# Linear attention followed by an MLP: the place of batch 3's v casts and key products inside chunk 2

## The chip, the cores and the metric

The kernel runs on one core of one Trainium2 chip. The metric is the device time of one execution in microseconds (us), median of several. A profile of one execution accompanies it: for every instruction it has the engine, the start, the length and what released it. Engines are named as in the profile: PE is TensorE's matmuls, PEld its weight loads, DVE is VectorE, ACT is ScalarE, POOL is GpSimd, SP is SyncE, which here only issues DMAs.

## The reference

Eight batches of eight heads, 576 rows, 64 columns a head. Attention without a square matrix: q is normalised by a softmax along its columns, k by a softmax along the sequence, and the product of k and v (64x64 for a head) is applied to q. The heads side by side give x (576 rows of 512), on which a layer norm, two matrix products with a ReLU between them and the residual follow.

```python
q_s = softmax(q, axis=-1)
k_s = softmax(k, axis=2)
kv  = einsum('bhsd,bhse->bhde', k_s, v)
x   = einsum('bhsd,bhde->bhse', q_s, kv)     # heads side by side: (8, 576, 512)
xn  = (x - mean(x)) / sqrt(var(x) + 1e-6) * g_ln
out = x + maximum(xn @ w_ch1, 0) @ w_ch2     # 512 -> 2048 -> 512
```

## The kernel before

**Chunks.** The MLP runs over chunks: chunk c is the first 512 rows of batch c, for c from 0 to 7, and a ninth chunk holds the remaining 64 rows of all eight batches. `mlp_steps(c)` gives the MLP of a chunk as a list of small TensorE steps, each with a weight, and `run(main, side)` (L846) issues them in order. `side` is a list of (position, function): before the main step at which the summed weight reaches that position, the function is issued. So the order on every engine is written out by hand, with positions from 0 to 112 in a chunk. A semaphore is waited for wherever an instruction needs another engine's result, and each engine takes its instructions strictly in that order.

**What is beside what.** While chunk c's MLP runs, the side list holds the attention of batch c + 1 (`attn_fast`, L877) and the loads and exponentials of batch c + 2 (`load_batch`, `load_v`, `prep_fast`).

**First product of a chunk** (`mm1_fast`, L753; chunks 2 and later). A Strassen-like scheme with seven products in place of eight. The 16 blocks of the hidden width are taken as four groups, two at a time. For each pair of groups the products come in the order 1, 5, 6, 2, 7, 3, 4; each has 4 matmuls for a group and weighs 2, so a pair takes 28 of the chunk's positions, and the two pairs take 0 to 56. Products 1, 6, 7 and 4 of a group share one PSUM bank (`bx`), 5 and 3 another (`bb`), 2 a third (`bc`), which begins as a copy of `bx`. Between them stand short operations:

- after product 5, ScalarE copies `bb` to SBUF (`s`, L778)
- after product 6, VectorE adds `bx` and `s` into `bb` (`add_5`, L781); product 7 writes `bx` again and so waits for it
- after product 7, VectorE adds `bx` and `s` into the hidden layer (`out_22`, L784), and after the second group of the pair it applies the ReLU to both (L789); product 4 writes `bx` again and so waits for L784
- after products 2, 3 and 4, ScalarE writes the ReLU of the bank to the hidden layer (L792)

Products 5, 6, 7 and 4 take differences of the transposed x, `tq`, which GpSimd forms (`sum_x`, L235 to L247) from `xnT` once a DMA has transposed `xn` (L255).

**Second product of a chunk** (`mm2_fast`, L684; positions 56 to 112), the same scheme over the hidden layer, with sums `hs` that VectorE forms (`sum_h`, L567).

**The attention of a batch.** `load_v(b)` (L139) loads v as bf16 into `vt`, of which there is one buffer, by a DMA on GpSimd's queue, and the remaining 64 rows into `vr`. `cast_v(b, j)` (L131) copies one half of the heads of `vt` into `vm`, where each head has a 65th column of ones, and which has one half for even and one for odd batches. `kv_all(b)` (L396) does the key products: `kv_mm` (L367) issues 40 matmuls of 64x65 into the PSUM tile `pkv`, the first 20 for heads 0 to 3, the others for heads 4 to 7; the 65th column is the sum that the softmax of k divides by. Then `kv_out` (L386) issues on VectorE a reciprocal (L390) and two multiplies (L392) that write `kv_sb`. From position 48 on `po_mm` (L417) multiplies q with it.

**Batch 3.** In most batches one cast is done by VectorE and one by ScalarE at the end of the chunk ahead. For batch 3 `load_v` is issued late in chunk 1 (L899), and both casts are done by VectorE in chunk 2, at positions 4 and 5 (L1186); its `kv_all` is at position 14 (L880), where that of later batches is at 12. `load_v(4)` is at position 26 of chunk 2 (L1183).

Of the kernel before, what the change touches and what calls it, by code (L numbers as in the profile page):

```python
# [20 lines left out]
def kernel(  # L21
# [109 lines left out]
    def cast_v(b, j, eng=None):  # L131
        hs = slice(4 * j, 4 * j + 4)
        dst = vm[:, b % 2, :, hs, 0:D].rearrange("p t h d -> p h t d")
        if eng is nc.scalar:
            nc.scalar.copy(dst, vts[b][:, hs])
        else:
            nc.vector.tensor_copy(out=dst, in_=vts[b][:, hs])
# [39 lines left out]
    def prep_kvrem(b):  # L177
        nc.scalar.activation(ekr[:, b % 2], raws[b][3], AF.Exp)
# [28 lines left out]
    def reduce_q(c, t, tn=1):  # L207
        ts = slice(t, t + tn)
        nc.vector.reduce_sum(eqs[c][1][:, ts], eqs[c][0][:, ts], axis=AX.X)  # L209
# [52 lines left out]
    def xn_T(c, t0, tn):  # L262
        dma_T(xnTs[c], xs[c][2][:, t0 : t0 + tn].rearrange("p t n -> p (t n)"), t0, tn)
# [103 lines left out]
    def kv_mm(b, ts):  # L367

        par = b % 2
        if ts.start == 0:  # L370
            kvbox["p"] = att_ps.tile([P, NP, P], FP32, tag="a", name="pkv")
        pkv = kvbox["p"]
        for jh, t in [(jh, t) for jh in range(2) for t in ts]:
            for j in (2 * jh, 2 * jh + 1):
                for half, ps in enumerate(halves):
                    h = 2 * j + half
                    if t < T:
                        lhsT, rhs = eks[b][:, t, h, :], vm[:, par, t, h, :]
                    else:
                        lhsT, rhs = ekr[:, par, h % 4, :], vr[:, par, h, :]  # L380
                    nc.tensor.matmul(  # L381
                        pkv[ps, j, 0:VW], lhsT, rhs, start=(t == 0 and j == 0), stop=(t == T),
                        skip_group_check=True,
                    )

    def kv_out(b):  # L386

        pkv = kvbox["p"]
        rzk = sml.tile([P, NP], FP32, tag="rzk", name="rzk")
        nc.vector.reciprocal(rzk, pkv[:, :, D])  # L390
        for ps in halves:
            nc.vector.tensor_mul(  # L392
                kv_sb[ps, b, :, ps], pkv[ps, :, 0:D], rzk[ps].to_broadcast([64, NP, D])
            )

    def kv_all(b):  # L396
        kv_mm(b, range(T + 1))
        kv_out(b)

    def start_x(c):  # L400
        xs[c] = (
            mlp.tile([P, T, DM], BF16, tag="x", name="x"),
            mlp.tile([P, T, 6], FP32, tag="st", name="st"),
            mlp.tile([P, T, DM], BF16, tag="xn", name="xn", bufs=1),
            mlp.tile([P, T, 2], FP32, tag="mv", name="mv"),
        )
        xnTs[c] = mlp.tile([P, T, KO1, P], BF16, tag="xnT", name="xnT")
# [36 lines left out]
    def x_fast(c, t, centre=True):  # L444

        x, _, _, mv = xs[c]
        nc.vector.scalar_tensor_tensor(  # L447
            x[:, t].rearrange("p (h d) -> p h d", h=H),
            in0=pobox[c, t].rearrange("p (h d) -> p h d", h=H), scalar=1.0,
            in1=eqs[c][2][:, t].to_broadcast([P, H, D]), op0=ALU.mult, op1=ALU.mult,  # L450
            accum_out=mv[:, t, 0:1],
        )
        if centre:
            xn_out(c, t)
# [387 lines left out]
    def spread(fns, a, b):  # L842
        n = len(fns)
        return [(a + (b - a) * i / n, fn) for i, fn in enumerate(fns)]
# [29 lines left out]
    def recip_q(c):  # L874
        nc.vector.reciprocal(eqs[c][2], eqs[c][1])

    def attn_fast(c):  # L877

        s = [(1, lambda: reduce_q(c, 0, 2)), (27, lambda: reduce_q(c, 2, 2)), (28, lambda: recip_q(c))]
        s += [(14 if c == 3 else 12, lambda: kv_all(c))]  # L880
        s += [(40, lambda: start_x(c))]
        for t, (p0, p1) in enumerate(((48, 53), (57, 59), (65, 67), (73, 75))):
            s += spread([lambda t=t, i=i: po_mm(c, t, i) for i in range(NP)], p0, p1)
            s += [(p1, lambda t=t: x_fast(c, t)), ((66, 74, 87, 91)[t], lambda t=t: square_sum(c, t))]
        s += [(61, lambda: xn_T(c, 0, 2)), (78, lambda: xn_T(c, 2, 2)), (95, lambda: rstd_op(c))]
        if c == C9 - 1:
            return s + [(100, lambda i=i: sum_x(c, i)) for i in range(2)]
        s += [((84, 88, 92, 101)[i], lambda i=i: sum_x(c, i)) for i in range(4)]
        return s
# [231 lines left out]
    with tc.manual_schedule(  # L1121
        engines={mybir.EngineType.PE, mybir.EngineType.DVE, mybir.EngineType.Activation,
                 mybir.EngineType.SP, mybir.EngineType.Pool}
    ):
        first_batch()
        load_behind(1, (2,))
        load_w2(8, 2)
        load_behind(1, (0,))
        load_w2(10, 2)
        load_behind(1, (1,))  # L1130
        load_w2(12, 2)
        load_w2(14, 2)
        load_behind(2)

        def po_x(c, t):
            for i in range(NP):
                po_mm(c, t, i)
            x_fast(c, t)

        run(  # L1140
            mlp_steps(0),
            [
                (2, lambda: (q0_rest(2), x_fast(0, 2))),
                (2.5, lambda: (eq_pT(0, 3, nc.scalar), x_plain(0))),
                (6, lambda: (q0_rest(3), x_plain(1))),
                (7.5, lambda: (xn_pT(0, 2, nc.vector), x_fast(0, 3))),
                (16, lambda: xn_pT(0, 3, nc.vector)),
                (22, lambda: square_sum(0, 0)),
                (26, lambda: square_sum(0, 1)),
                (30, lambda: square_sum(0, 2)),  # L1150
                (34, lambda: square_sum(0, 3)),
                (38, lambda: rstd_op(0)),
            ]
            + [(70, lambda: exp_q(1, 0, 4)), (72, lambda: exp_q(1, 2, 4))]
            + [(75 + t, lambda t=t: reduce_q(1, t)) for t in range(T)]
            + [((82, 86, 94, 98)[t], lambda t=t: eq_pT(1, t, nc.scalar)) for t in range(T)]
            + [(84, lambda: nc.vector.reciprocal(eqs[1][2], eqs[1][1]))]
            + [(88, lambda: exp_k(1, 0, 4)), (92, lambda: exp_k(1, 2, 4))]
            + [(26 + 4 * i, lambda i=i: scale_w1(i % KO1, i // KO1)) for i in range(2 * KO1)]
            + [(p, lambda i=i: quarter_w2(i, 0)) for i, p in enumerate((60, 62, 64, 66))]  # L1160
            + [(p, lambda i=i: sum_w1(i, 0)) for i, p in enumerate((80, 84, 88, 92))]
            + [(p, lambda i=i: sum_w1(i, 1)) for i, p in enumerate((96, 98))]
            + [(103 + 0.4 * j, lambda j=j: cast_v(1, j)) for j in range(2)]
            + [(104.5, lambda: prep_kvrem(1))]
            + [(112, lambda: (kv_all(1), start_x(1)))]
            + [(118, lambda: (po_x(1, 0), po_x(1, 1)))]
            + [(123, lambda: xn_pT(1, 0, nc.scalar)), (125, lambda: square_sum(1, 0))]
            + [(124.1, lambda: (po_x(1, 2), po_x(1, 3)))]
            + [(126, lambda: xn_pT(1, 1, nc.scalar)), (127, lambda: square_sum(1, 1))]
        )  # L1170
        for c in range(1, B):
            side = []
            if c == 1:
                side += second_side()
            else:
                if c + 1 < B:
                    side += attn_fast(c + 1)
                else:
                    side += attn_rest()
                    side += [(6 + i, lambda i=i: sum_x(c, i)) for i in (2, 3)]  # L1180
                if c + 2 < B:
                    side += [(1, lambda b=c + 2: load_batch(b))]
                    side += [(26, lambda b=c + 2: load_v(b))]  # L1183
                    side += prep_fast(c + 2)
            if c == 2:
                side += [(4 + j, lambda j=j: cast_v(3, j)) for j in range(2)]  # L1186
            if c == B - 2:
                side += [(1, load_qrem)]
                side += spread([lambda r=r: exp_qrem(r) for r in range(T)], 58, 80)
                side += [(84, lambda: eq_T(C9))]  # L1190
            sums = [(57, 0)] if c == FAST else [(p, i) for i, p in enumerate((30, 41))]
            run(mlp_steps(c), side + [(at, lambda i=i: sum_h(0, i)) for at, i in sums])
        run(mlp_steps(C9), [(33 + 3 * i, lambda i=i: sum_h(0, i)) for i in range(2)])
# [30 lines left out]
```

## Time and profile before

| | |
|---|---|
| runs | 264.39, 264.46, 265.11 us; median 264.46 us |
| profiled execution | 266.13 us, of which the span from first to last instruction is 264.3 us |
| granted TensorE clock | 1.000 of full speed |
| VectorE, ScalarE, GpSimd busy | 218.0, 180.8, 78.3 us |
| DMA | 45.00 MB, mean 170 GB/s |
| chunk 2, first to last of its TensorE work | 76.49 to 104.78 us |
| chunk 3 | 104.78 to 130.99 us |

The page has the busy time of each engine (matmuls are pipelined, each is given its modelled length of 0.27 us for 128x256 although the next one starts 0.11 us later), the chain of work that ended last, and the costliest groups of instructions. The trace behind it answers finer questions: the timeline of one engine in a window, the waits by length, one tile's instructions. An instruction is named by its line, its operation and out<-in. Neighbouring VectorE and ScalarE instructions overlap by about 0.09 us in the records.

### The profile page before, as it was taken

To read this page: it belongs to the slowest core of one execution; us is meant where nothing else is said; L and a number is where in the kernel's file an instruction comes from. 1 tells how busy PE (TensorE), PEld (TensorE's weight loads), DVE (VectorE), ACT (ScalarE), POOL (GpSimd) and SP (SyncE) were. 2 spreads that over 40 slices of the span, in tenths; PEclk is the share of its full clock that TensorE was granted. 3 is DMA by queue.
4 is the path that set the end of the run, shared out by engine and by line. 5 is a ranking of instruction groups with operands and counts; after the bars stand their busy time and mean duration, and the time that the engine had idled before them with its cause. 6 is when DMAs were issued, how large, how long until landed. Compare 5 with 4: busy or idle time off the path is not lost.

```text
span 264.3 us, 6846 instructions
## 1 busy us (share of the span) xinstructions
PE 256.2 (97%) x2711; PEld 217.1 (82%) x2711; DVE 218.0 (82%) x482; ACT 180.8 (68%) x357; POOL 78.3 (30%) x130
## 2 busy tenths in 40 slices
PE   8989999999997999999999999999999999999993
PEld 6778755866886998899889988998899888888882
DVE  4767686988968997989798979897989899977873
ACT  4867671996964888688868886888688378437400
POOL 8651336200089006700670059007300300030000
PEclk9999999999999999999999999999999999999999
DMA  6999999995999956699679986997903720521014
GB/s 218 257 202 206 323 230 307 269 139 184 263 154 254 298 81 122 174 307 151 117 191 308 142 109 179 324 147 145 263 13 69 173 83 2 79 94 68 0 42 119
DMA packets 69895, 45.00 MB, mean 170 GB/s; under 512 B 41508, under 2 KB 66088, under 8 KB 69864
## 3 DMA queue, kind: packets, MB, share of 16 engines
q1 hardware_dynamic: 48896, 21.76, 39.0%
q0 software_dynamic: 20368, 22.29, 38.9%
q10 hardware_dynamic: 600, 0.53, 0.6%
q8 instruction: 21, 0.34, 0.5%
q14 instruction: 10, 0.08, 0.1%
HBM read 36.70 MB, written 9.44 MB: 175 GB/s over the span
## 4 chain that ended last, share of the span: by engine, by line
PE 85%; DMA 9%; DVE 2%; POOL 1%; issue 1%; ACT 0%; POOLq 0%; DVEq 0%
PE ba L598 18%; PE bx L750 18%; PE bb L750 9%; PE ph L501 8%; PE pc L547 5%; PE bb L598 5%; PE be L598 5%; PE bc L598 5%; PE bc L750 4%; DMA qt<-in_q_dram 4%; DMA xnT<-xn 3%; PE ph L486 3%; PE po L417 2%; DMA vt<-in_v_dram 2%; PE pkv L381 2%; PE ptr L933 1%
## 5 line engine op out<-in xcount | busy, mean ns | idle before, releaser
L598 PEld LDWEIGHTS <-hs 128*128 128x128 bf16 x512 | 49.6, 98 | 5.7
L750 PEld LDWEIGHTS <-w_q 128*128 128x128 bf16 x448 | 43.2, 98 | 5.0
L598 PEld LDWEIGHTS <-hT 128*128 128x128 bf16 x392 | 37.4, 98 | 4.4
L750 PEld LDWEIGHTS <-w1g 128*128 128x128 bf16 x336 | 32.1, 98 | 4.4 <-DVE hT L784 0.4
L247 POOL TENSOR_TENSOR tq<-xnT 128x256 bf16<-128x256 bf16 x20 | 13.0, 667 | 66.2 <-DMA xnT<-xn 50.1
L598 PE MATMUL ba<-w_q,hs 128*128 128x256 bf16 x256 | 31.7, 273 | 0.0
L615 POOL DMA_DIRECT2D out_dram<-ot x28 | 15.5, 566 | 46.0 <-DVE ot L609 46.0
L750 PE MATMUL bx<-tq,w_q 128*128 128x256 bf16 x224 | 29.0, 273 | 0.0
L431 ACT ACTIVATE scrap<-x,mv 128x512 bf16<-128x512 bf16 x36 | 26.0, 722 | 1.8 <-DVE x L447 1.4
L792 ACT ACTIVATE hT<-bc 128x512 bf16<-128x512 f32 x28 | 15.4, 595 | 13.5 <-PE bc L750 13.5
L447 DVE SCALAR_TENSOR_TENSOR x<-po,rq 128x512 bf16<-128x512 f32 x34 | 23.3, 685 | 1.4 <-PE po L417 1.3
L774 ACT COPY bc<-bx 128x512 f32<-128x512 f32 x28 | 15.2, 593 | 13.0 <-PE bx L750 13.0
L781 DVE TENSOR_TENSOR bb<-bx,s 128x512 f32<-128x512 f32 x28 | 18.1, 693 | 6.0 <-ACT s L778 5.8
L209 DVE TENSOR_REDUCE zq<-eq 128x16 f32<-128x1024 bf16 (+1 forms) x20 | 20.8, 1051 | 1.4 <-ACT eq L192 1.1
L578 DVE TENSOR_TENSOR hs<-hT 128x1024 bf16<-128x1024 bf16 x32 | 20.9, 674 | 0.9 <-ACT hT L792 0.5
L792 ACT ACTIVATE hT<-bb 128x512 bf16<-128x512 f32 x28 | 15.2, 595 | 8.5 <-PE bb L750 8.5
L417 PE MATMUL po<-kv_sb,eqT 128*128 128x128 bf16 x120 | 20.2, 219 | 0.0
L784 DVE TENSOR_TENSOR hT<-bx,s 128x512 bf16<-128x512 f32 x28 | 18.0, 684 | 2.5 <-PE bx L750 2.5
L623 ACT COPY s<-ba 128x512 f32<-128x512 f32 x15 | 8.7, 578 | 11.9 <-PE ba L598 7.3
L598 PE MATMUL ba<-w_sb,hT 128*128 128x256 bf16 x128 | 16.7, 273 | 0.0
L598 PE MATMUL bb<-w_q,hs 128*128 128x256 bf16 x128 | 16.5, 273 | 0.0
L192 ACT ACTIVATE eq<-qt 128x1024 bf16<-128x1024 f32 x14 | 14.6, 1057 | 1.3 <-DMA qt<-in_q_dram 1.3
(150 smaller groups left out, 544.9 us busy)
## 6 DMA issues: line engine op xcount, KB each, us to landing
out_dram<-ot POOLq DMA_DIRECT2D x32, 256.0 KB, 6.0
qt<-in_q_dram SPq DMA_DIRECT2D x5, 1024.0 KB, 6.5
kt<-in_k_dram SPq DMA_DIRECT2D x5, 1024.0 KB, 13.0
vt<-in_v_dram POOLq DMA_DIRECT2D x7, 512.0 KB, 13.4
qt<-in_q_dram POOLq DMA_DIRECT2D x2, 1024.0 KB, 12.7
kt<-in_k_dram POOLq DMA_DIRECT2D x2, 1024.0 KB, 14.7
kt<-in_k_dram SPq DMA_DIRECT2D x4, 288.0 KB, 4.9
w_raw<-in_moe_w_ch_dram POOLq DMA_DIRECT2D x4, 256.0 KB, 10.1
```

Of the source, the lines that this page charges most:

```text
L209: nc.vector.reduce_sum(eqs[c][1][:, ts], eqs[c][0][:, ts], axis=AX.X)
L417: nc.tensor.matmul(pobox["p"][:, i * P : i * P + P], eqTs[c][:, t, i, :], kv_sb[:, c, i, :], start=True, stop=True,)
L431: nc.scalar.activation(scrap, x[:, t], AF.Square, bias=mv[:, t, 0:1], scale=-float(DM), accum_out=mv[:, t, 1:2],)
L447: nc.vector.scalar_tensor_tensor(x[:, t].rearrange("p (h d) -> p h d", h=H), in0=pobox[c, t].rearrange("p (h d) -> p h d", h=H), scalar=1. ...
L501: nc.tensor.matmul(ph[:, m % 2, at : at + tn], (w1g if c else w1_sb)[:, ko, m * P : (m + 1) * P], xnTs[c][:, t0 : t0 + tn, ko, :], start=( ...
L578: nc.vector.tensor_tensor(out=dst, in0=x, in1=y, op=op)
L598: nc.tensor.matmul(dst, lhsT, rhs, start=first and (own or t == 0) and k == 0, stop=k == KH - 1, skip_group_check=True)
L615: nc.gpsimd.dma_start(out[c, 0:SM, :].rearrange("(p t) n -> p t n", t=T)[:, t], ybox[c, t])
L750: nc.tensor.matmul(dst[:, q], lhsT, rhs, start=first and q == 0 and ko == 0, stop=ko == 1, skip_group_check=True)
L781: nc.vector.tensor_tensor(out=at[g, "b"], in0=at[g, "x"], in1=at[g, "s"], op=ALU.add)
L784: nc.vector.tensor_tensor(out=h_out(g, 1, 1), in0=at[g, "x"], in1=at[g, "s"], op=ALU.add)
L792: nc.scalar.activation(h_out(g, odd, half), at[g, name], AF.Relu)
```

## The change

The two casts of batch 3's v move from positions 4 and 5 of chunk 2 to 19 and 20, and batch 3's `kv_all` from position 14 to 34. Everything else keeps its position.

```diff
     def attn_fast(c):
 
         s = [(1, lambda: reduce_q(c, 0, 2)), (27, lambda: reduce_q(c, 2, 2)), (28, lambda: recip_q(c))]
-        s += [(14 if c == 3 else 12, lambda: kv_all(c))]
+        s += [(34 if c == 3 else 12, lambda: kv_all(c))]
         s += [(40, lambda: start_x(c))]
...
             if c == 2:
-                side += [(4 + j, lambda j=j: cast_v(3, j)) for j in range(2)]
+                side += [(19 + j, lambda j=j: cast_v(3, j)) for j in range(2)]
```

On TensorE the 40 key matmuls stood between product 2 of group 0 and that of group 1; now they stand between product 5 of group 2 and that of group 3. On VectorE the order in the first part of chunk 2 was and is (each line from left to right):

```
before: cast 0, cast 1, L781 x2, L390, L392 x2, L784, L784, L789, reduce, reciprocal, hs, L781 x2, hs
after:  L781 x2, L784, cast 0, L784, L789, cast 1, reduce, reciprocal, hs, L390, L392 x2, L781 x2, hs
```

## The prediction

> **What bounds the kernel now.** I read the page first, then the chain of waits, then the timelines of TensorE and VectorE where the chain leaves TensorE.
>
> ```profile
> PE 256.2 (97%) x2711; PEld 217.1 (82%) x2711; DVE 218.0 (82%) x482; ACT 180.8 (68%) x357; POOL 78.3 (30%) x130
> PE 85%; DMA 9%; DVE 2%; POOL 1%; issue 1%; ACT 0%; POOLq 0%; DVEq 0%
> ```
>
> TensorE is busy for 97% of the span and carries 85% of the chain that ends last, so an edit is worth what it takes away from TensorE's idle time. Little of that is left. From 84.36 us to the end the chain is almost all TensorE; the last stretch of other work before that is this one (chain of waits from 73 us; columns are start, length, what):
>
> ```profile
> 73.55 6.41 DMA vt<-in_v_dram
> ...
> 80.99 0.42 DVE vm L137
> 81.41 1.20 DVE bb L781 x2
> ...
> 82.72 0.42 DVE kv_sb L392
> 83.15 0.43 DVE kv_sb L392
> 83.58 0.03 issue
> 83.61 0.70 DVE hT L784
> 84.31 0.05 issue
> 84.36 2.06 PE bx L750 x16
> ```
>
> Batch 3's v lands at 73.55 + 6.41 = 79.96 us; two casts, two adds, the output of the key products and one ReLU addend follow on VectorE, and TensorE waits for them twice. The timelines of TensorE and then of VectorE show where (start, length, instruction, in brackets the idle time before it):
>
> ```profile
> 78.35 1.03 PE L750 MATMUL bx<-tq,w_q 128*128 128x256 bf16 x8
> 79.22 0.60 PE L750 MATMUL bc<-xnT,w1g 128*128 128x256 bf16 x4
> 81.13 0.44 PE L381 MATMUL pkv<-vm,ek 128*64 128x65 bf16 x16 [1.31 <-DVE vm L137]
> ...
> 83.22 1.04 PE L750 MATMUL bb<-xnT,w_q 128*128 128x256 bf16 x8
> 84.36 1.19 PE L750 MATMUL bx<-tq,w1g 128*128 128x256 bf16 x8
> 85.38 1.04 PE L750 MATMUL bx<-xnT,w1g 128*128 128x256 bf16 x8
> ```
>
> ```profile
> 80.05 1.36 DVE L137 COPY vm<-vt 128x1024 bf16<-128x1024 bf16 x2 [1.35 <-DMA vt<-in_v_dram]
> 81.32 1.28 DVE L781 TENSOR_TENSOR bb<-bx,s 128x512 f32<-128x512 f32 x2
> ```
>
> Eight matmuls of this kind follow each other in 0.87 us in chunk 3 (starts 109.85 and 110.72 there), four in 0.44. So the four `bc` from 79.22 are issued by 79.66 and the next matmul starts at 81.13: 1.47 us lost (the bracket's 1.31 counts from the modelled end). From 83.22 to 84.36 is 1.14 in place of 0.87: 0.27 lost. From 84.36 to 85.38 is 1.02: 0.15 lost. Together 1.89 us. As a check, chunk 2 runs from 76.49 to 104.78 (28.29 us) and chunk 3 from there to 130.99 (26.21 us), 2.08 more; 0.12 of the rest is the gap ahead of 78.35, which waits for GpSimd's `tq` and which the edit leaves.
>
> **What the edit moves.** Nothing is added or removed: 2 casts, 40 key matmuls, 1 reciprocal and 2 multiplies of the key output change places, and no DMA is issued elsewhere by the program. On TensorE the 40 matmuls go from between the two `bc` groups (step 14) to between the two `bb` groups of the second half (step 34). On VectorE the order becomes: adds, first L784, cast 0, second L784, L789, cast 1, reduce, reciprocal, sum of hT, key output, adds of the second half.
>
> **TensorE without the wait**, from 79.66 at chunk 3's rate: second `bc` to 80.09, product 7 80.09 to 80.97 (first group to 80.53), product 3 to 81.84, product 4's first group to 82.28. Their `tq` inputs end at 79.53 (product 7) and 80.77 (product 4) on GpSimd: margins 0.56 and 1.07 us.
>
> **VectorE.** Its last work ahead of the casts ends at 78.70, so it can add as soon as product 6 is done. The 4th and the 8th matmul from 78.35 end (0.33 and 0.76 to their start, 0.27 each) at 78.95 and 79.38; the adds run about 79.05 to 80.33 (1.28 in the row above), ahead of product 7's second group at 80.53. The first L784 comes 0.64 after product 7's start (108.97 to 109.61 in chunk 3), so 80.73, and takes 0.69, to 81.42. Cast 0: the tile's view gives casts 419 ns at least, 424 in the middle, 1021 at most, the last being the row at 80.05, whose partner at 80.99 took 0.42. I take 0.42, because the long one lay under GpSimd's `tq` sums, over at 80.77, and cast 0 now starts at 81.33 (0.09 overlap between neighbours, as between those two). It ends at 81.75, the second L784 at 82.35. TensorE, 0.05 behind as at 84.31 to 84.36, starts product 4's second group at 82.40 in place of 82.28: **new wait 0.12 us**. Queued behind it on TensorE is everything, so that counts in full.
>
> Then L789 (0.43) to 82.81, cast 1 to 83.14. TensorE ends product 4 at 82.84, runs product 1 to 83.71 and half of product 5 to 84.15, and the key matmuls find both casts 1.0 us old. They cost 0.77 as before (81.13 to 81.90), to 84.92, `bb` to 85.36, product 6 to 86.23, product 2 to 87.10. VectorE meanwhile: reduce 1.20, reciprocal 0.35, sum 0.63, to 85.19; key reciprocal and output (0.17 + 0.86) to 86.16; adds 86.19 to 87.48. Product 7's two groups, at 87.10 and 87.54, need them at 86.89 and 87.48 plus 0.05: margins 0.16 and 0.01. Sum (0.68) and both L784 end at 89.28; product 3 with its 4 `po` matmuls (1.10, from 89.75 to 90.85 before) brings product 4 to 89.08 where it was at 90.85. **Sum: 1.89 - 0.12 = 1.77 us less**; the exhausted margin of 0.01 makes me take 1.7.
>
> **Does the gain last?** What is late next must not be a transfer with a date of its own. Batch 4's loads go out at the same place: k (79.25, landing at 91.91) is used at 98.31, v (83.13, 11.9 us to landing) at 100.45, margins over 5 us. The next v load on GpSimd's queue waits for cast 1, now 83.14, so the issue at 83.13 moves by some 0.1 and its two `vr` loads with it; they write batch 4's half of `vr`, so the key products of batch 3, which now stand behind them in the program, need not wait for them. SyncE's queue is passed by nothing that moves. From 86 us on TensorE has no gap worth naming, and chunks 3 to 7 follow as now. Without any of this cover the price is that of the third rival.
>
> [...] The row: cast 0 took 1021 ns beside GpSimd's sums, cast 1 419 beside a store issue that then took 811 ns where the next ones took 577, 557 and 552, and L789 took 652 at 84.93 beside a `vr` load issue against 426 to 428 elsewhere. [...]
>
> **The rivals.**
> - *VectorE becomes the bound, because the casts run long.* For it: the 1021 and 652 ns above, GpSimd busy from 80.72 to 85.33, margins of 0.16 and 0.01. Against: 419 ns beside a store. If each takes 0.65 (0.23 more), the new wait is 0.35, and the gain 1.54: 262.9 us. If each takes 1.02 (0.60 more), product 4 waits 0.72, and the adds end 1.20 later against a TensorE 0.60 later, 0.43 more at product 7: gain 0.74, 263.7 us. Middle 263.3.
> - *The change does not do what it says:* cast 0 still meets a v that has not landed, and VectorE's queue stands as before. That needs the landing after 81.33. v loads took 6.4 to 15.2 us to landing, this one 6.41; but nothing ahead of 79 us changes. Gain lost, about 264.4 us.
> - *Slower: xnT's transposes of batch 3 catch batch 4's loads.* They are issued at 94.77 and 97.97, as batch 4's v lands (83.13 + 11.9 = 95.0), and would go 1.7 earlier, the first of them beneath that load. A transpose under loads at 64.79 took 7.3 us to land and held SyncE for 3.93. Two in a row like that land at 93.07 + 3.93 + 7.3 = 104.3, GpSimd's first `tq` pair (1.30) ends at 105.6, and product 5 of chunk 3, due at 105.49 - 1.7 = 103.8, starts 1.8 late; the second pair comes 1.26 behind the first where TensorE needs it 0.87 behind, 0.4 more. 264.46 - 1.7 + 2.2 = 265.0 us. It decides once the second lands after 102.5 (103.8 less 1.30); now it lands at 97.97 + 3.3 = 101.3. Against: in chunk 3 the first goes out at 121.07 beneath the loads of batch 5 (the next v load, 108.62, takes up to 15.2 us), the second at 124.19 lands 3.4 us later, and chunk 4 starts without a gap.
>
> **How the numbers follow.** The profiled execution took 266.13 us, 264.3 of it span; the medians shown come from other executions, 264.46, 0.6% below it. The 1.7 us comes off each: span 262.6, median **262.75**. Chances: forecast 0.72, its own range 262.3 to 263.1; long casts 0.14; no gain 0.07; transposes 0.07. Range 262.2 to 264.2: it holds the first two, and leaves out the last two and a little below. A difference of 0.3% (0.8 us) is about the least that this measurement can tell. Faster by more: 0.72 and 0.10 of the long casts, 0.82; the same: 0.04 and 0.07, 0.11; slower: 0.07.
>
> **What would show it.** Right: no idle time ahead of `pkv` in chunk 2; two casts of about 0.42 at 81.3 and 82.7; a gap of about 0.1 inside the first product 4; the second product 4 at 89.1; chunk 3 from about 103.1, every later chunk 26.2 long. Wrong: casts near 1 us, a gap ahead of product 7 near 87.5, a v that lands later, or idle time ahead of `bb` at the start of chunk 3 with GpSimd waiting for xnT.

## The result and the profile after

The changed kernel takes 263.92 us in the median of 22 runs (263.30 to 265.02), the kernel before 265.31 us in 22 runs beside them (263.99 to 266.73). The ratio is 0.995, 95% interval 0.9932 to 0.9967: 1.39 us less, between 0.9 and 1.8. A second measurement with other executions of both, further below, gives 0.9934 (0.9907 to 0.9961), 1.66 us less. The profiled execution took 264.16 us with a span of 262.4 us, against 266.13 and 264.3 before.

The first view is three stages of each profiled execution: ahead of chunk 2's first TensorE work, chunk 2, and the rest. Columns: stretch and its length, busy time and instructions of PE, PEld, DVE, ACT and POOL, granted clock, DMA share, GB/s. The kernel before:

```profile
0.00:76.49 76.49, 74.23 (x823) 55.23 (x824) 57.81 (x144) 54.28 (x110) 29.65 (x52) 1.00 1.10 232
76.49:104.62 28.13, 26.73 (x283) 23.39 (x281) 24.63 (x52) 20.89 (x39) 12.05 (x20) 1.00 0.93 194
104.62:264.30 159.68, 155.27 (x1610) 138.51 (x1607) 135.54 (x288) 105.66 (x208) 36.60 (x60) 1.00 0.62 137
```

The changed kernel:

```profile
0.00:75.65 75.65, 74.47 (x824) 55.49 (x825) 57.72 (x144) 54.23 (x110) 29.38 (x51) 1.00 1.10 233
75.65:102.66 27.01, 26.66 (x283) 23.42 (x280) 23.91 (x52) 20.76 (x39) 12.15 (x20) 1.00 0.98 205
102.66:262.40 159.74, 155.28 (x1610) 138.49 (x1607) 135.58 (x288) 105.67 (x208) 36.84 (x61) 1.00 0.61 137
```

The chain that ended last now holds 92% TensorE and 3% DMA, where it was 85% and 9%; the changed kernel's page:

```profile
PE 256.4 (98%) x2711; PEld 217.4 (83%) x2711; DVE 217.2 (83%) x482; ACT 180.7 (69%) x357; POOL 78.4 (30%) x130
PE 92%; DMA 3%; POOL 1%; DVE 1%; issue 1%; ACT 0%; POOLq 0%; DVEq 0%
```

The rest after chunk 2 is the same to 0.06 us: what chunk 2 gains is kept. Chunk 2 is 1.12 us shorter, and 0.84 us more lies ahead of it, where no instruction was moved; that part differs from execution to execution. So does the time from the start of chunk 2 to its product 2, below called the front: 2.73 us before and 3.29 here, which hides 0.56 of the gain. Within chunk 2 TensorE's timeline shows where the time went (start, length, instruction, idle time before it):

```profile
78.07 1.03 PE L750 MATMUL bx<-tq,w_q 128*128 128x256 bf16 x8 [0.21 <-ACT s L778]
78.94 1.04 PE L750 MATMUL bc<-xnT,w1g 128*128 128x256 bf16 x8
79.81 1.04 PE L750 MATMUL bx<-tq,w_q 128*128 128x256 bf16 x8
80.69 1.04 PE L750 MATMUL bb<-xnT,w_q 128*128 128x256 bf16 x8
81.56 1.16 PE L750 MATMUL bx<-tq,w1g 128*128 128x256 bf16 x8
82.56 1.04 PE L750 MATMUL bx<-xnT,w1g 128*128 128x256 bf16 x8
83.43 0.60 PE L750 MATMUL bb<-tq,w_q 128*128 128x256 bf16 x4
83.96 0.45 PE L381 MATMUL pkv<-vm,ek 128*64 128x65 bf16 x16
...
84.72 0.61 PE L750 MATMUL bb<-tq,w_q 128*128 128x256 bf16 x4
```

From product 2 on everything follows at 0.87 us for eight matmuls, but for product 4 (81.56 to 82.56, 0.13 more) and the start of the key products (due 0.44 after 83.43, 0.09 late). No wait for v is left. VectorE beside it:

```profile
80.45 0.69 DVE L784 TENSOR_TENSOR hT<-bx,s 128x512 bf16<-128x512 f32 x1 [0.39 <-PE bx L750]
81.06 0.42 DVE L137 COPY vm<-vt 128x1024 bf16<-128x1024 bf16 x1
81.39 0.68 DVE L784 TENSOR_TENSOR hT<-bx,s 128x512 bf16<-128x512 f32 x1
82.11 0.43 DVE L789 TENSOR_SCALAR hT<-hT 128x1024 bf16<-128x1024 bf16 x1
82.45 0.47 DVE L137 COPY vm<-vt 128x1024 bf16<-128x1024 bf16 x1
```

v landed at 79.67 us, 1.4 ahead of cast 0, and cast 1 ends at 82.92, 1.0 us ahead of the key products. In the chain of waits these are now ordinary TensorE work:

```profile
83.60 0.44 PE bb L750 x4
84.03 0.76 PE pkv L381 x40
84.79 0.54 PE bb L750 x4
```

A measure free of what happens ahead of the change is the time from the first matmul of product 2 to the first of the second pair's product 4: 11.63 us before (79.22 to 90.85), 9.95 after (78.94 to 88.89). In these two executions the change itself is worth 1.68 us. This stretch is used below. Without any wait it would be 11.63 - 1.89 = 9.74 by the prediction's reading; 0.09 of the 1.89 turns out to be no wait, which makes it 9.83, and run 3 below shows 9.82.

### The profile page after: what moved, and what is told of

It is laid out like the page before. It is cut to its first block, busy times and chain, and to the rows that moved or that the text cites. A ratio compares the mean times of both kernels' runs of the same rounds, so it can differ in the third digit from the quotient of the medians.

```text
span 262.4 us, 6846 instructions
## 1 busy us (share of the span) xinstructions
PE 256.4 (98%) x2711; PEld 217.4 (83%) x2711; DVE 217.2 (83%) x482; ACT 180.7 (69%) x357; POOL 78.4 (30%) x130
## 4 chain that ended last, share of the span: by engine, by line
PE 92%; DMA 3%; POOL 1%; DVE 1%; issue 1%; ACT 0%; POOLq 0%; DVEq 0%
PE ba L598 19%; PE bx L750 18%; PE bb L750 9%; PE ph L501 8%; PE pc L547 5%; PE bc L750 5%; PE bc L598 5%; PE be L598 5%; PE bb L598 5%; DMA xnT<-xn 3%; PE ph L486 3%; PE warm L864 3%; PE po L417 2%; PE pkv L381 2%; PE ptr L933 1%
## 5 line engine op out<-in xcount | busy, mean ns | idle before, releaser
L778 ACT COPY s<-bb 128x512 f32<-128x512 f32 x28 | 15.6, 622 | 0.6 <-PE bb L750 0.5
```

The source lines that it names most:

```text
L778: nc.scalar.copy(at[g, "s"], at[g, "b"])
```

## Experiments

The ratio compares each run with executions of the kernel before that were taken beside it (median 265.50 us for runs 1 to 4, 265.61 for 5 to 8, 265.58 for 9 to 12), so it is not the quotient of the medians. The stretch comes from one profiled execution of each.

| run | stretch, us | time, us | ratio to before, 95% interval |
|---|---|---|---|
| changed kernel | 9.95 | 263.92 | 0.995 (0.9932 to 0.9967) |
| 1 key products alone | 11.96 | 265.62 | 1.0039 (1.001 to 1.0067) |
| 2 casts alone | 11.23 | 265.20 | 0.9993 (0.9969 to 1.0017) |
| 3 before, v loaded earlier | 9.82 | 265.36 | 1.0004 (0.9977 to 1.0031) |
| 4 changed, v loaded earlier | 9.95 | 264.78 | 0.9987 (0.9963 to 1.0012) |
| 5 key products at 28 | 10.06 | 264.22 | 0.9952 (0.9924 to 0.9981) |
| 6 key products at 22 | 11.21 | 265.18 | 0.9992 (0.9964 to 1.002) |
| 7 casts at 20 | 9.91 | 263.93 | 0.9942 (0.9918 to 0.9965) |
| 8 changed, v loaded later | 21.44 | 274.75 | 1.0342 (1.0302 to 1.0382) |
| 9 changed, small loads first | 9.95 | 264.08 | 0.9961 (0.993 to 0.9992) |
| 10 before, small loads first | 10.43 | 265.55 | 1.0005 (0.9974 to 1.0036) |
| 11 before again | 11.64 | 265.62 | 0.9981 (0.9946 to 1.0016) |
| 12 changed again | 9.95 | 263.92 | 0.9934 (0.9907 to 0.9961) |

### Each half of the change alone

Run 1, the key products alone:

```diff
-        s += [(14 if c == 3 else 12, lambda: kv_all(c))]
+        s += [(34 if c == 3 else 12, lambda: kv_all(c))]
```

> Batch 3's key products move to position 34 as in the change, the casts stay at 4 and 5. Theory (the gain is the wait of TensorE for batch 3's v, and it ends only when neither TensorE's key products nor VectorE's adds stand behind the casts): the adds still stand behind the casts and end at 82.01 and 82.61, so product 7, due at 80.09 without the key products ahead of it, starts near 82.06: 1.97 us lost there, 0.16 at its second group, against 1.89 lost before. Time about 0.2 us above the kernel before, and a gap of some 2 us ahead of product 7 in place of the one ahead of the key products. Rival (moving the key products is what gains): as fast as the changed kernel, 1.4 us (0.5%) below before.

Measured: no gain, rather a small loss. TensorE's timeline, and then VectorE's, of run 1:

```profile
79.47 1.04 PE L750 MATMUL bc<-xnT,w1g 128*128 128x256 bf16 x8
82.33 1.19 PE L750 MATMUL bx<-tq,w_q 128*128 128x256 bf16 x8 [1.82 <-DVE bb L781]
83.36 1.04 PE L750 MATMUL bb<-xnT,w_q 128*128 128x256 bf16 x8
```

```profile
80.32 1.35 DVE L137 COPY vm<-vt 128x1024 bf16<-128x1024 bf16 x2 [1.88 <-DMA vt<-in_v_dram]
81.58 1.28 DVE L781 TENSOR_TENSOR bb<-bx,s 128x512 f32<-128x512 f32 x2
```

With the casts still at the head of VectorE's queue, the adds wait for v behind them, and product 7 waits for the adds: 82.33 in place of 79.47 + 0.87 = 80.34, 1.99 us lost (1.97 expected), and 0.16 at its second group (0.16 expected). TensorE no longer waits for the casts at all, and it costs more than before.

Run 2, the casts alone, just behind the adds:

```diff
-                side += [(4 + j, lambda j=j: cast_v(3, j)) for j in range(2)]
+                side += [(12.1 + j / 10, lambda j=j: cast_v(3, j)) for j in range(2)]
```

> The casts move behind the two adds of the first pair (position 12.1), the key products stay at 14. Theory: the adds end at 80.33, the casts follow at 80.24; the key products wait for the first one. If that cast takes 0.42, 1.05 us are lost in place of 1.47, and the losses of 0.27 and 0.15 behind it go: 0.8 us gained over before. If it again runs beside GpSimd's sums and takes 1.0, 1.6 us are lost and 0.3 gained. Rival (the casts' place alone makes the gain): 1.4 us below before.

Measured: the stretch is 0.40 us shorter, the time not distinguishable from before. TensorE's timeline of run 2:

```profile
78.64 0.60 PE L750 MATMUL bc<-xnT,w1g 128*128 128x256 bf16 x4
80.56 0.44 PE L381 MATMUL pkv<-vm,ek 128*64 128x65 bf16 x16 [1.32 <-DVE vm L137]
```

The key products start 1.48 us late as before, and only the losses of 0.27 and 0.15 behind them are gone. The first cast took 844 ns beside GpSimd's sums, the case for which 0.3 us was expected. So neither half gains what both do: 0.40 for the casts, minus 0.33 for the key products, 1.68 together.

### v's date

Run 3 (order of before) and run 4 (changed order) let v's load wait for batch 3's q in place of batch 2's transposed xn:

```diff
-        s += [(60.5, lambda: load_v(3, xnTs[2][0:1, 1, KO1 - 1, 0:4]))]
+        s += [(60.5, lambda: load_v(3, raws[3][2][0:1, 0, 0, 0:4]))]
```

> The order of before, but batch 3's v load waits for batch 3's q to land (67.1 us) in place of batch 2's transposed xn (72.1), so it is issued some 4 to 5 us earlier. Theory: v lands before 78 us, the casts at position 4 and 5 run at once at 78.7 for 0.84, the key products find the first cast done at 79.2, and the wait of 1.47 and the losses behind it are gone: 1.5 to 2 us below before, as long as the transposes of batch 2 and k of batch 3 do not come late for sharing the DMA engines; if they do, a gap appears ahead of chunk 2 or in the second product of chunk 1, and the gain is smaller by it. Rival (the order on VectorE, not v's date, costs the time): within 0.3 us of before.

> The changed kernel with the same earlier v load. Theory: v's date no longer decides anything, so within 0.3 us of the changed kernel (1.2 to 1.9 below before), up to 0.3 better because GpSimd's sums for chunk 2 no longer stand behind the load's issue. Rival (the changed kernel still waits for v somewhere): a further 0.5 us or more below the changed kernel.

Measured: v lands at 75.50 us in run 3, and the stretch falls to 9.82 with the order of before. With v there in time, the order of before waits nowhere in the stretch. But the time does not fall. TensorE's timeline of run 3:

```profile
75.85 1.04 PE L750 MATMUL bx<-xnT,w1g 128*128 128x256 bf16 x8
78.50 1.03 PE L750 MATMUL bb<-tq,w_q 128*128 128x256 bf16 x8 [1.62 <-POOL tq L247]
80.12 1.03 PE L750 MATMUL bx<-tq,w_q 128*128 128x256 bf16 x8 [0.59 <-POOL tq L247]
```

Product 5 waits for `tq`. The transpose of the second half of xn, issued at 68.12 beside v's load, lands at 77.02 us, 8.9 later, where it takes 3.3 to 5.0 us in the runs in which v's load waits for the first half, and `tq` is late with it. The gain of 1.81 in the stretch is paid back as 5.15 us from the start of chunk 2 to product 2, where 2.62 is the time without a wait. Run 4 shows a price without the gain: its stretch is 9.95, as in the changed kernel, so an earlier v no longer helps there, and its front takes 3.83 us. Of the 1.3 us between the two fronts, 0.9 is the transpose, which lands 1.2 us after chunk 2's start in run 3 and 0.2 in run 4; the other 0.4 is the second pair of `tq` sums, which took 1.65 us beside the casts in run 3 and 1.28 in run 4. I expected the time of run 4 within 0.3 us of the changed kernel; it is 0.9 above it, with 1.2 us lost in the front. This also shows that the danger named in the prediction, a transpose that meets loads, is real. The changed kernel's own transposes of batch 3 did not come late (the slower rival in the account below).

Run 8 issues v's load behind chunk 2's `tq` sums:

```diff
-        s += [(60.5, lambda: load_v(3, xnTs[2][0:1, 1, KO1 - 1, 0:4]))]
+        s += [(109, lambda: load_v(3, xnTs[2][0:1, 1, KO1 - 1, 0:4]))]
```

> The changed kernel with batch 3's v load issued on GpSimd's queue behind the four tq pairs of chunk 2, so near 79.4 in place of 73.5; v then lands some 6.4 to 12 us later, at 86 to 91. Theory: TensorE waits at the second group of product 4 until the landing plus 1.2 us (0.1 to the cast, 0.42 cast, 0.69 L784 less overlap, 0.05), where it is due at about 82.2: 5 to 10 us lost, and the margin that the changed kernel has is the 1.4 us between landing (79.7) and cast 0 (81.06). At its front the wait of product 6 for tq is gone (0.1 to 0.2 us). Rival (v's date does not matter to the changed kernel at all, as a mere reordering gains): within 0.5 us of the changed kernel.

Measured: v lands at 90.42 us, and the second group of product 4 starts 1.17 us later, at 91.59:

```profile
81.42 0.60 PE L750 MATMUL bx<-tq,w1g 128*128 128x256 bf16 x4
91.59 1.01 PE L750 MATMUL bx<-tq,w1g 128*128 128x256 bf16 x4 [9.58 <-DVE hT L784]
92.40 1.91 PE L750 MATMUL bx<-xnT,w1g 128*128 128x256 bf16 x8
```

So the changed order still depends on v, by a chain of the expected length (landing plus 1.2), but only once v lands later than about 1.4 us behind where it does. The stretch is 11.49 us longer than the changed kernel's; the wait is 9.73 of it, the rest is in the last section.

v's landing is not all that sets the date of the casts in the order of before. In four traces (the kernel before, runs 1, 2 and 11) cast 0 ended 7.53 to 7.54 us after v's load was issued, although v had landed after 6.4 to 6.6. It ended behind a `tq` sum that GpSimd had queued behind that load, and took 844 to 1021 ns in place of 420. So 0.4 to 0.6 us of TensorE's wait of about 1.5 is owed to the sum, the rest to the landing.

### Where the key products and the casts can stand

Runs 5 and 6 move the key products of the changed kernel to 28 and to 22, run 7 its casts to 20 and 20.1:

```diff
-        s += [(34 if c == 3 else 12, lambda: kv_all(c))]
+        s += [(28 if c == 3 else 12, lambda: kv_all(c))]
...
-                side += [(19 + j, lambda j=j: cast_v(3, j)) for j in range(2)]
+                side += [(20 + j / 10, lambda j=j: cast_v(3, j)) for j in range(2)]
```

> The changed kernel with the key products at position 28 in place of 34. Theory (any place behind the casts' end is as good): TensorE gets there 82.84 on the clock of before, the first cast is done at 81.75, the second at 83.14, needed at 83.18, so no wait: within 0.3 us of the changed kernel, no gap above 0.1 us ahead of the key products. Rival (the place between the two product 5 groups is itself what gains): 0.5 us or more slower than the changed kernel.

> The changed kernel with the key products at position 22, between the two groups of product 3. Theory: TensorE is there at 81.40, waits 0.40 for the first cast and, after 20 matmuls, 1.05 for the second (83.19): 1.45 us lost, 0.12 of product 4's wait saved, so 1.3 us slower than the changed kernel and 0.4 below before. Rival (the casts' new place alone gains): as fast as the changed kernel.

> The changed kernel with both casts behind both L784 and the ReLU (positions 20 and 20.1). Theory: the new wait of 0.12 to 0.13 us at the second group of product 4 goes, all else stays: 0.1 us below the changed kernel, which only the trace can show (product 4 of the first pair takes 0.87 in place of 1.00). Rival (that wait is not the cast's): product 4 still takes 1.00.

Measured: at 28 the stretch is 10.06 and the time 264.22, no different from the changed kernel. At 22 TensorE comes too early for both casts (run 6):

```profile
81.51 0.44 PE L381 MATMUL pkv<-vm,ek 128*64 128x65 bf16 x16 [0.25 <-DVE vm L137]
81.79 0.23 PE L381 MATMUL pkv<-vr,ekr 128*64 128x65 bf16 x4
82.90 0.45 PE L381 MATMUL pkv<-vm,ek 128*64 128x65 bf16 x16 [0.88 <-DVE vm L137]
```

It starts 0.40 late (due at 80.67 + 0.44 = 81.11) and waits once more for cast 1, and the stretch is 11.21: 1.26 more than the changed kernel where 1.3 was expected. Of the 20 positions by which the key products moved, those up to the casts' end are needed, the others are not.

Run 7 removes the wait inside product 4 (81.16 to 82.03, the normal 0.87) but gains only 0.04 in the stretch. Its VectorE adds of the second pair run from 85.57 to 86.87, and product 7, whose second group is due at 86.39 + 0.44 = 86.83, takes 1.12 where it takes 1.04 elsewhere: 0.08 is handed back there. The 0.13 of the changed kernel is the cast's, but VectorE is so nearly the bound in this half of the chunk that taking it away buys next to nothing; the times are equal (263.93 and 263.92).

### What differs from execution to execution

Runs 11 and 12 repeat both kernels, for their traces. Runs 9 and 10 issue batch 3's two small loads (`vr`) ahead of GpSimd's wait for xn, in the changed order and in the order of before:

```diff
         if after is not None:
+            load_vr(b)
             nc.gpsimd.tensor_copy(out=vts[b][0:1, 0, 0, 0:4], in_=after)
...
-        for half in range(2):
+        if after is None: load_vr(b)
+    def load_vr(b):
+        for half in range(2):
```

> The changed kernel, with batch 3's two small loads (vr) issued by GpSimd ahead of its wait for batch 2's transposed xn in place of behind v's load; tq of chunk 2 is then formed 1.3 us sooner after v's issue. Theory: the front of chunk 2 (start to product 2) loses what v's issue later than 3.05 us ahead of the chunk's start costs (traces so far: issue 2.94, 2.58, 2.43, 2.37 and 2.21 us ahead, loss 0.11, 0.47, 0.61, 0.68 and 0.84; 3.73 ahead, none), because tq stands behind the two vr issues on GpSimd. In the changed kernel nothing behind hides that loss, so it is gained in full: front at 2.62 us, 0.3 to 0.8 us below the changed kernel in the median, if the small loads do not make the transposes land later. Rival (the front's wait has another cause): within 0.2 us of the changed kernel.

> The kernel before with the same edit to GpSimd's queue. Theory: TensorE's wait ahead of the key products ends with v's landing whatever the front does, so the front's loss goes and the wait at the key products grows by as much: the second pair's product 4 still starts 10.9 us behind v's landing (79.96 to 90.85 before), and the time is within 0.3 us of before. Rival (the two losses add): 0.3 to 0.8 us below before, as in the changed kernel.

> The kernel before once more, for its trace. Theory: how far ahead of chunk 2 v's load is issued differs from execution to execution, and here the sum of the front's loss and the wait at the key products is about 4.5 us less that lead (4.52 - 2.94 = 1.58 in the first trace), down to none for a lead of 4.5 us; product 4 of the second pair starts 10.9 us behind v's landing as long as there is such a wait. Time as before.

> The changed kernel once more, on the same chip as the others. Theory: product 2 to the second pair's product 4 again 9.95 us, whatever the front loses (0 to 0.9 us) and whenever v lands up to 1.4 us later; time 1.0 to 1.7 us below before.

Measured: the stretch repeats to 0.02 us (11.64 and 9.95). TensorE's timeline of the kernel before, second execution (run 11):

```profile
77.81 1.03 PE L750 MATMUL bx<-tq,w_q 128*128 128x256 bf16 x8 [0.16 <-POOL tq L247]
78.68 0.60 PE L750 MATMUL bc<-xnT,w1g 128*128 128x256 bf16 x4
80.60 0.44 PE L381 MATMUL pkv<-vm,ek 128*64 128x65 bf16 x16 [1.32 <-DVE vm L137]
```

v's load went out 2.73 us ahead of chunk 2 (its lead), the front lost 0.32 and the key products 1.48, together 1.80, where 4.52 - 2.73 = 1.79 was expected. Product 4 of the second pair, however, started 10.75 us behind v's landing and not 10.9 (10.89 in the first trace). Behind the issue of v's load it started 17.30 and 17.31 us: the wait follows GpSimd's queue and not the landing. In run 12 the lead was 4.35 us and the front lost nothing.

The gain is therefore not the same in every execution. The traces of the order of before have leads of 2.4 to 2.9 us, or 3.0 with the small loads first (run 3 apart, which moves the load). With a lead of 4.35 its wait of 1.48 at the key products would be some 0.2 (an estimate: 1.48 less the 1.30 by which the lead passes 3.05, where the front stops losing). No trace shows that case; the differences of the medians, 1.39 and 1.66 us, are over whatever leads occurred.

Run 9's front takes 2.62 us as expected, but its time, 264.08, is that of the changed kernel (263.92), where 0.3 to 0.8 less was expected. Part of the reason lies outside the program's work: in runs 9 and 10 every execution takes 2.12 to 2.21 us more than its span from first to last instruction, in all others 1.74 to 1.92. The median span of run 9 is 261.9 us and that of run 12 262.1, so at most 0.2 was saved in the span, which is within the noise, and some 0.37 lost outside it. Why the edit costs that is open, and so is why the front's saving is so small in the median. Run 10's time is that of before, as expected, but not for my reason. Its wait does not grow, it shrinks. VectorE's timeline of run 10:

```profile
78.65 0.77 DVE L137 COPY vm<-vt 128x1024 bf16<-128x1024 bf16 x2 [0.63 <-DMA vt<-in_v_dram]
```

The key products are 0.27 late in place of 1.47. Half of that 1.20 is the cast: GpSimd's last sum ends at 78.78, and cast 0 takes 0.43 in place of 1.02, so that the second pair's product 4 starts 10.30 us behind the landing and not 10.89. The other half is the landing, 0.13 us after product 2 begins in place of 0.74. In that one execution the span is 262.4 us; the median span of its 12 runs is 263.4, 0.4 below that of the kernel before beside it (263.8), and about as much is lost again outside the span. Why the traced execution is 1.0 us below the median is open: no trace of a typical one was taken. I found no version that beats the changed kernel beyond the intervals.

## Why the prediction was right

The forecast was 1.7 us less, by the wait for batch 3's v going off TensorE. The runs give 1.39 (0.9 to 1.8) and 1.66, the trace 1.68 in the stretch that holds all that was moved. Runs 1, 2 and 6 show that the wait stays when either queue still meets it.

- *The wait and its size.* Of the 1.89 us read as lost, the stretch shows 1.68 gained. The new wait of 0.12 at product 4 measures 0.13. The other 0.09 is the start of the key products, late by as much where nothing is waited for. That is the one term mis-sized: the 1.47 held 0.09 that belongs to any place of these products (in chunk 3 of the kernel before they also start at 107.33, 0.10 behind 106.36 + 0.87), so the sum of 1.77 should have been 1.68; rounding down to 1.7 hid it. The prediction's check against chunk 3 could not show it, because 104.78 is a date of the chain of waits and 76.49 one of the timeline: by the timeline chunk 2 takes 28.13 us (76.49 to 104.62), 1.92 more than chunk 3, which is 1.80 and the 0.12 ahead of 78.35.
- *VectorE's order.* Cast 0 was due at 81.33 on the clock of before and started at 81.06, with product 2 itself 0.28 earlier (78.94 for 79.22). Casts of 422 and 465 ns stand for the 0.42 assumed. The adds of the second pair ended at 87.27, in time for product 7's second group at 87.36, as the margin of 0.01 had it: a margin that thin held by luck.
- *The rival of long casts* did not come about. The line's view in the changed kernel (count, then shortest, middle and longest in ns) has 422 and 465 ns beside store issues, and the casts take 413 to 497 in all runs in which they stand at 19 or behind.

```profile
L137 DVE COPY vm<-vt x2: 422/444/465, 81.1 to 82.5; 128x1024 bf16<-128x1024 bf16 x2
```

  What lay beside VectorE in the kernel before, from GpSimd's and VectorE's timelines (its first cast ran from 80.05 to 81.07):

```profile
79.49 1.28 POOL L247 TENSOR_TENSOR tq<-xnT,tq 128x256 bf16<-128x256 bf16 x2
84.03 1.30 POOL L149 DMA_DIRECT2D vr<-in_v_dram  x2
84.93 0.65 DVE L789 TENSOR_SCALAR hT<-hT 128x1024 bf16<-128x1024 bf16 x1
```

  In five traces a cast ended 0.28 to 0.30 us after a `tq` sum that ran beside it (80.77 and 81.07, 81.04 and 81.33, 80.22 and 80.51, 80.25 and 80.54, and in run 3 78.45 and 78.75), whatever its own start: its end went with the sum's. Beside GpSimd's DMA issues only some ran longer. In the traces of the two kernels nine casts and ReLUs (L789) began during one. The ReLU above began 0.27 us into it and ended 0.25 behind it (85.58 after 85.33, 652 ns in place of 427); cast 1 of the changed kernel began 0.33 into one and ended 0.25 behind it (465 ns). Three that began 0.52 to 0.66 into one took their usual 426 ns and ended 0.30 to 0.41 behind it, and four that began 0.03 to 0.27 into one took 419 to 427 and ended ahead of its end. What decides is not shown: cast 1 of the kernel before began as far into a store issue as that ReLU into its `vr` issue and took 419 ns, while the issue took 811 in place of 552 to 577.

  Part of the gain is just this: the casts were taken out from under the sums. That they went so well is in part luck, since they now stand beside the stores:

```profile
80.45 2.21 POOL L615 DMA_DIRECT2D out_dram<-ot  x4
```

  Cast 0 started at 81.06, 0.03 us into a store's issue, and cast 1 0.33 us into one, for which it paid 0.05. A cast 0 drawn out as the ReLU was in the kernel before would take about 0.65 (an estimate from the ReLU's 652 ns), which is the first price of that rival.
- *The rival that v lands too late* has its point where the prediction put it: landing against cast 0, 1.4 us apart, and run 8 shows what lies beyond.
- *The slower rival*, transposes beneath loads: the first went out at 93.04 under v's load (landed 94.24) and landed after 3.1 us, the second at 96.20 after 3.3. Runs 3 and 4 show that those of batch 2 can cost 1.2 us and more when a load is put beside them.
- *The level.* The predicted 262.75 stood on the median of three runs, 264.46. Over 22 runs that median is 265.31, so the time came out 1.2 above the point although the difference was 0.3 off. At 263.92 it lies in the stated range of 262.2 to 264.2, but above the 262.3 to 263.1 that the prediction gave for its own forecast, and nearer to the rival of long casts. By the time alone that rival would have looked right; the traces decide against it. That the wider range held the time, with a base off by 0.85, is luck.

## What to carry to other kernels

A wait that shows on one engine may be held by two queues at once. Here TensorE's own products and VectorE's adds both stood behind the late transfer, and in the stretch moving either alone gained 0.4 us or lost 0.3, both together 1.7. Follow the late transfer through every in-order queue that it blocks and move what depends on it behind the work that does not, just so far that the input is ready when the engine gets there. Look also at what runs on GpSimd beside a VectorE copy: here cast 0 took 0.76 to 1.02 us beside GpSimd's sums in five traces, in place of 0.42. Before loading the late operand earlier, look at what its load was kept away from.

## What the runs showed of the hardware that was not expected

After run 8's wait of 9.6 us TensorE came back at half its clock. Columns as in the stages above, the clock third from the end:

```profile
82.00:91.50 9.50, 0.01 (x1) 0.00 (x0) 0.99 (x2) 0.75 (x2) 1.35 (x3) 0.68 1.24 277
91.50:93.50 2.00, 1.91 (x10) 1.31 (x10) 1.93 (x5) 0.60 (x1) 0.87 (x1) 0.50 0.68 275
93.50:95.50 2.00, 2.00 (x23) 1.26 (x22) 0.89 (x2) 1.44 (x3) 1.31 (x3) 0.50 0.64 59
95.50:98.00 2.50, 2.50 (x52) 2.26 (x47) 1.74 (x5) 0.87 (x2) 0.00 (x0) 0.97 1.46 175
```

Eight matmuls take 1.71 us (92.40 to 94.11) in place of 0.87, for some 4 us, which adds 11.49 - 9.73 = 1.8 us to the wait. If the clock went from 1.00 to 0.50 once, its mean of 0.68 over 9.50 us puts that 3.4 us into the wait; in the same way the 0.97 of the last row puts the return at about 95.65, 4.1 us after TensorE's restart at 91.59. Both dates are estimates, from the mean clocks around one wait. The wait of 1.3 us before the change, with a granted clock of 1.00 from 78 to 84 us, had no such tail.
